# Sigmoid attention and a SiLU layer on one core: later loads for batch 3, a ring of three v tiles, and other places for scores

## The chip, the core and the metric

The kernel runs on one core of a Trainium2 chip. The metric is the device time of one execution in microseconds (us); the median of three runs of the kernel before is 384.71 us (383.19 to 385.27). Engines are named as in the profile: PE (TensorE), PEld (its weight loads), DVE (VectorE), ACT (ScalarE), POOL (GpSimd), SP (SyncE). POOL and SP only issue DMAs here, but for a few small set-up operations.

## The reference

q, k, v are float32 of shape (8, 12, 448, 64): batch, heads, sequence, head size. w_in is (768, 2048), w_out (2048, 768).

```
scores = q @ k^T / sqrt(64) - log(448)
attn   = sigmoid(scores)
x      = (attn @ v), heads put side by side: (8 * 448, 768)
h      = x @ w_in
out    = (h * sigmoid(h)) @ w_out          # (3584, 768), float32
```

## The kernel before

**Blocks and units.** The 12 heads of a batch are taken four at a time, so a batch is three blocks and all batches are 24 blocks, g = 0 to 23; batch b has blocks 3b to 3b + 2. A block has seven units, one for each chunk of 64 keys, 168 units in all. `scores` (line 171) does one unit: four matmuls of 64 rows by 64 columns of the array (psc, line 178) and one ScalarE sigmoid (attnT, line 185). PSUM holds two score tiles. `values` (line 195) multiplies a block's seven attnT tiles by v: 28 matmuls (pav, line 209) and two copies on DVE into x^T (xT, line 220).

**The layer.** `h_unit` (line 229) makes 128 of the 2048 hidden columns of a batch, called fc: six matmuls (ph), a sigmoid (tsig, line 245) and a product on DVE (gTr, line 246). `out_set` (line 286) multiplies two row blocks of gTr by w_out in seven products of eight matmuls (po, line 303) instead of eight products, by sums and differences of the operands (S on DVE, lines 315 to 323; the sums of w_out are `w_sums`, line 264). Its results go to osb tiles on DVE and from there by four stores on SP (line 296). `all_moe` (line 376) is the order of all this: h of batches 0 and 1, three sets; h of batch 2, a set, h of batch 3, two sets and one more; and so on.

**Order on PE.** There is no scheduler: instructions run in the order written. The main loop (line 528) emits a burst of two units of scores, then the values of a block if one waits, then one row copy if one is due (`rows_if_any`), then a stretch of the layer (`stretch`, line 395), which takes steps from the generator `all_moe` until their nominal nanoseconds reach what is due. Each step is one matmul. Unit n = 42 is batch 2's first, and ahead of it stands one long stretch of 21500 ns, in which h of batch 1 is done with no scores between.

**k^T and q^T.** The scores need k and q transposed. Blocks 0 to 5 are transposed on PE. From block 6 on, `dma_transpose` (line 160) copies a flat tile to rows (kr, qr) and issues a DMA transpose on SP (line 165) to kT or qT. For blocks 6 to 8 the copies are done on ACT inside h of batch 1, behind the fc units that `by_h1` (line 351) names. For later blocks they are done on DVE (line 164), one to a burst, out of the list `later` that `after_values` fills.

**Loads.** POOL issues all loads of k, q, v (`load`, line 72: two halves of 112 KB for each tensor and block), of w_in in four quarters and of w_out in four quarters, in the order in which the functions `after_transpose` (line 425) and `after_values` (line 443) call for them. A load waits on POOL until its tile is free, and all later loads stand behind it. Eight loads can be under way: each instruction also waits for the landing of the load eight places earlier. The flat tiles of k and q are rings of four, that of v a ring of five (pool p5). `load("kq", g)` in `moe_h` (line 364) and in `rows_if_any` (line 466) fetches the block four further on, right behind a transpose's copies.

Of the kernel before, what the change touches and what calls it, by code (L numbers as in the profile page):

```python
# [17 lines left out]
def kernel(  # L18
# [21 lines left out]
    NFC = DFF // P  # L40
    NO2 = DMODEL // 2
    NQB = NQ * B
# [7 lines left out]
    p2 = ctx.enter_context(tc.tile_pool(name="p2", bufs=2))  # L50
    p3 = ctx.enter_context(tc.tile_pool(name="p3", bufs=3))
    p4 = ctx.enter_context(tc.tile_pool(name="p4", bufs=4))
    p5 = ctx.enter_context(tc.tile_pool(name="p5", bufs=5))
    p12 = ctx.enter_context(tc.tile_pool(name="p12", bufs=12))
    ps_sc = ctx.enter_context(tc.tile_pool(name="ps_sc", bufs=2, space=bass.MemoryType.PSUM))
    ps_1 = ctx.enter_context(tc.tile_pool(name="ps_1", bufs=4, space=bass.MemoryType.PSUM))
# [8 lines left out]
    flat = {}  # L65

    def new_flat(name, g):
        flat[name, g] = (p5 if name == "v" else p4).tile(
            [P, 2, NCH, D], F16, tag=f"{name}f", name=f"{name}f"
        )  # L70

    def load(names, g, c0=0, c1=NCH):
        b, iq = divmod(g, NQ)
        for name in names:
            if (name, g) not in flat:
                new_flat(name, g)
            for half in range(2):
                h0 = half * (H // 2) + 2 * iq
                nc.gpsimd.dma_start(  # L79
                    flat[name, g][half * HP : (half + 1) * HP, :, c0:c1].rearrange(  # L80
                        "p i c d -> p i (c d)"
                    ),
                    source[name][b, h0 : h0 + 2].rearrange("i (p c) d -> p i (c d)", c=NCH)[
                        :, :, c0 * D : c1 * D
                    ],
                )
# [20 lines left out]
    def load_w_in(step):  # L107
        cols = slice(step * DFF // 4, (step + 1) * DFF // 4)
        nc.gpsimd.dma_start(  # L109
            w_in_sb[:, :, cols], moe_w_in[:, cols].rearrange("(cc p) f -> p cc f", p=P)  # L110
        )

    def load_w_out(nh, part):
        cols = slice(nh * NO2, (nh + 1) * NO2)
        fcs = slice(part * NFC // 2, (part + 1) * NFC // 2)
        nc.gpsimd.dma_start(
            w_out_sb[:, fcs, cols],
            moe_w_out[part * DFF // 2 : (part + 1) * DFF // 2, cols].rearrange(
                "(fc p) e -> p fc e", p=P
            ),  # L120
        )
# [104 lines left out]

    pairs = [half * NQ + iq for iq in range(NQ - 1) for half in range(2)] + [NQ - 1, 2 * NQ - 1]

    def h_unit(b, fc):
        ph = ps_1.tile([P, 512], F32, tag="ps1", name="ph")  # L230
        for at, cc in enumerate(pairs):
            assert b in ready or at < 4
            nc.tensor.matmul(  # L233
                ph[:, :S],
                w_in_sb[:, cc, fc * P : (fc + 1) * P],
                xT[b][:, cc, :],
                start=(at == 0),
                stop=(at == NCC - 1),
            )
            if at < NCC - 1:  # L240
                yield 189
        if fc == NFC - 1:
            h_done.add(b)
        tsig = p3.tile([P, S], F16, tag="tsig", name="tsig")
        nc.scalar.activation(tsig, ph[:, :S], AF.Sigmoid, bias=0.0, scale=ISX)  # L245
        nc.vector.tensor_mul(  # L246
            gTr[:, fc, (b % 2) * S : (b % 2) * S + S], ph[:, :S], tsig
        )
        yield 189
# [34 lines left out]
        return [rows_of[2 * m + u // NCH, u % NCH] for u in (2 * g, 2 * g + 1)]  # L284

    def out_set(a1, rows1, a2, rows2, last=False):
        lo, hi = slice(0, NHC), slice(NHC, NFC)
        osb = [p4.tile([P, DMODEL], F32, tag="osb", name="osb") for _ in range(2)]
        c11, c12 = (osb[0][:, nh * NO2 : (nh + 1) * NO2] for nh in range(2))
        c21, c22 = (osb[1][:, nh * NO2 : (nh + 1) * NO2] for nh in range(2))  # L290
        m1 = p2.tile([P, NO2], F32, tag="m1", name="m1")
        sg = [cpool.tile([P, NHC, P], F16, tag=f"S{i}", name=f"S{i}") for i in range(1, 5)]

        def store(rows, o, cols, engines):
            for at, (row, eng) in enumerate(zip(rows, engines)):
                eng.dma_start(row[:, cols], o[at * HP : (at + 1) * HP, cols])

        left, right, whole = slice(0, NO2), slice(NO2, DMODEL), slice(0, DMODEL)

        def product(a, w):  # L300
            po = ps_1.tile([P, 512], F32, tag="ps1", name="po")
            for fc in range(NHC):
                nc.tensor.matmul(  # L303
                    po[:, :NO2], a[:, fc, :], w[:, fc, :], start=(fc == 0), stop=(fc == NHC - 1)
                )
                if fc < NHC - 1:
                    yield 163
            return po[:, :NO2]

        def plus(o, po, x, sign=ISX):  # L310
            nc.vector.scalar_tensor_tensor(  # L311
                out=o, in0=po, scalar=sign, in1=x, op0=ALU.mult, op1=ALU.add
            )

        nc.vector.tensor_sub(sg[2], a1[:, lo], a2[:, lo])  # L315
        nc.vector.tensor_add(sg[0], a2[:, lo], a2[:, hi])
        po = yield from product(a1[:, lo], wq[0][0])
        nc.scalar.activation(m1, po, AF.Copy, scale=ISX)  # L318
        nc.vector.tensor_sub(sg[1], sg[0], a1[:, lo])
        yield 163  # L320
        po = yield from product(a1[:, hi], wq[1][0])
        plus(c11, po, m1)
        nc.vector.tensor_sub(sg[3], a1[:, hi], sg[1])
        if last:
            store(rows1, osb[0], left, (nc.sync, nc.sync))
        yield 163
        po = yield from product(sg[2], tw[3])
        plus(c22, po, m1)
        yield 163
        po = yield from product(sg[1], tw[2])  # L330
        plus(c22, po, c22)
        plus(c12, po, m1)
        yield 163
        po = yield from product(a2[:, hi], tw[4])
        plus(c21, po, c22, -ISX)
        yield 163
        po = yield from product(sg[0], tw[1])
        plus(c22, po, c22)
        plus(c12, po, c12)
        store(rows2, osb[1], whole, (nc.sync, nc.sync))  # L340
        yield 163
        po = yield from product(sg[3], wq[1][1])
        plus(c12, po, c12)
        if last:
            store(rows1, osb[0], right, (nc.sync, nc.scalar))
        else:
            store(rows1, osb[0], whole, (nc.sync, nc.sync))
        yield 163


    by_h1 = {4: 6, 7: 7, 10: 8}
    early = [h_unit(0, fc) for fc in range(2)]
    sums = w_sums()

    def moe_h(b):
        for fc in range(NFC):
            yield from early[fc] if b == 0 and fc < 2 else h_unit(b, fc)
            if b == 1:
                if fc >= 2:
                    next(sums)  # L360
                if fc in by_h1:
                    for name in ("k", "q"):
                        dma_transpose(by_h1[fc], name, act_copy)
                    load("kq", by_h1[fc] + 4)

    def moe_set(m, g):
        step = out_set(block(g), row_blocks(m, g), block(g + 1), row_blocks(m, g + 1))
# [25 lines left out]
    done = due = 0.0  # L393

    def stretch(ns):
        nonlocal done, due
        due += ns
        while done < due:
            step_ns = next(stream, None)
            if step_ns is None:  # L400
                break
            done += step_ns
# [19 lines left out]
    units = [(g, ch) for g in range(NQB) for ch in range(NCH)]  # L422
    waiting = []

    def after_transpose(g):
        if g == 0:
            load("kq", 4)
            load_w_in(1)
        elif g == 1:
            load("kq", 5)  # L430
            load_w_in(2)
            load("v", 3)
            load_w_in(3)
            load("v", 4)
        elif g == 4:
            load("kq", 8)
            load("v", 6)
            load("v", 7)
        elif g == 5:
            load("v", 8)  # L440
            load("kq", 9)

    def after_values(g):
        if g == 0:
            load("v", 5)
            for nh in range(2):
                for part in range(2):
                    load_w_out(nh, part)
        elif g == 2:
            load("kq", 6)  # L450
            load("kq", 7)
        elif g >= 4 and g + 5 < NQB:
            load("v", g + 5)
        if g >= 6:
            for to in (9, 10) if g == 6 else (g + 4,):
                if to < NQB:
                    later.extend(((to, "k"), (to, "q")))

# [2 lines left out]
    def rows_if_any():  # L461
        if later:
            g, name = later.pop(0)
            dma_transpose(g, name, nc.vector.tensor_copy)
            if name == "q" and g + 4 < NQB:
                load("kq", g + 4)

    def values_if_any():
# [110 lines left out]
```

## Time and profile before

| what | value |
|---|---|
| median of three runs | 384.71 us |
| the profiled execution: time / span | 386.89 / 385.1 us |
| granted TensorE clock | 1.000 |
| PE busy / ACT / DVE / POOL | 373.2 / 240.1 / 233.5 / 93.0 us |
| matmuls ph, po (four forms of operands and kept), psc, pav | 768, 784, 672, 672 |
| DMA queue 0 (POOL's loads) / queue 1 (SP's) | 22.69 MB / 19.31 MB |
| DMA transposes on SP | 36, kT landing after 7.5 us, qT after 7.0 us (medians) |
| POOL's longest wait in total | vf behind PE pav, 98.2 us in 12 |

The span runs from the first to the last instruction; the time of the profiled execution is a little longer. "Busy" of PE counts modelled ends of pipelined matmuls. The chain of work that ended last follows back, from the last instruction, to what released each step; a DMA in it was waited for. In a timeline, the brackets at a line's end tell how long the engine was idle and who ended it, and a trailing q ("SPq") marks an issue, not work. The DMA share is the mean busy share of 16 DMA engines; it passes 1 where packets overlap.

### The profile page before, as it was taken

Reading aid. Unit: us, or ns where it says so; the run is one execution under the profiler, and the core shown is the slowest. Engines: PE = TensorE matmul, PEld = TensorE weight load, DVE = VectorE, ACT = ScalarE, POOL = GpSimd, SP = SyncE. Lnnn points to the kernel's source line nnn. Section 1 sums busy time; section 2 is a strip of 40 time slices with the busy share of each in tenths; the row PEclk is TensorE's granted clock in tenths of the full one; section 3 lists DMA queues with packets and bytes.
Section 4 is the critical chain, followed back from the end, with each engine's and each line's share of the span. In section 5 each row is a group of like instructions: output and inputs, shape, how many; then the busy total and the mean of one; then the engine's idle time right before and its main releaser. Section 6 shows DMA issues by size and latency. Waiting matters only on the chain.

```text
span 385.1 us, 7662 instructions
## 1 busy us (share of the span) xinstructions
PE 373.2 (97%) x3083; PEld 186.8 (48%) x3083; DVE 233.5 (61%) x415; ACT 240.1 (62%) x328; POOL 93.0 (24%) x158
## 2 busy tenths in 40 slices
PE   7998999997999999999999999999999999999995
PEld 2543445553544444444555444544455444555663
DVE  2445646894685656655767546745757444756774
ACT  4998685856766886678454587577874686044000
POOL 8953516541344313221312301101000000000000
PEclk9999999999999999999999999999999999999999
DMA  7999999999999999928949764445131300110233
GB/s 111 181 190 205 205 203 170 153 130 119 195 108 210 147 212 112 171 53 98 98 107 201 68 137 73 39 115 73 24 69 40 83 3 0 26 57 2 67 98 82
DMA packets 66403, 42.71 MB, mean 111 GB/s; under 512 B 37056, under 2 KB 62912, under 8 KB 66368
## 3 DMA queue, kind: packets, MB, share of 16 engines
q0 software_dynamic: 28032, 22.69, 45.0%
q1 hardware_dynamic: 38112, 19.31, 30.1%
q8 instruction: 24, 0.39, 0.4%
q10 hardware_dynamic: 224, 0.23, 0.2%
q14 instruction: 11, 0.09, 0.1%
HBM read 45.61 MB, written 11.01 MB: 147 GB/s over the span
## 4 chain that ended last, share of the span: by engine, by line
PE 83%; DMA 8%; ACT 5%; POOL 1%; issue 1%; DVE 1%; ACTq 0%; POOLq 0%
PE ph L233 36%; PE po L303 31%; PE psc L178 9%; PE pav L209 7%; ACT attnT L185 5%; DMA qT<-qr 4%; DMA vf<-in_v_dram 3%; DMA kf<-in_k_dram 1%; POOL qf L79 1%; DVE gTr L246 0%; ACT tsig L245 0%; PE ptrk L149 0%; POOL w_in_sb L109 0%; DVE S L315 0%; POOL vf L79 0%
## 5 line engine op out<-in xcount | busy, mean ns | idle before, releaser
L185 ACT ACTIVATE attnT<-psc,bias_s 128x896 f16<-128x896 f32 x168 | 159.1, 1015 | 57.7 <-PE psc L178 57.7
L233 PE MATMUL ph<-xT,w_in_sb 128*128 128x448 f16 x768 | 153.6, 353 | 0.0
L246 DVE TENSOR_TENSOR gTr<-ph,tsig 128x448 f16<-128x448 f32 x128 | 78.1, 623 | 75.3 <-ACT tsig L245 74.5
L233 PEld LDWEIGHTS <-w_in_sb 128*128 128x128 f16 x768 | 71.8, 98 | 76.2 <-issue 13.6
L245 ACT ACTIVATE tsig<-ph 128x448 f16<-128x448 f32 x128 | 68.2, 545 | 49.9 <-PE ph L233 49.0
L303 PEld LDWEIGHTS <-S 128*128 128x128 f16 x448 | 42.1, 98 | 34.5 <-issue 6.7
L79 POOL DMA_DIRECT2D vf<-in_v_dram x48 | 28.7, 615 | 104.7 <-PE pav L209 98.2
L311 DVE SCALAR_TENSOR_TENSOR osb<-po,osb 128x384 f32<-128x384 f32 x70 | 37.7, 555 | 26.7 <-PE po L303 26.1
L178 PE MATMUL psc<-qT,kT 64*64 64x448 f16 x672 | 50.4, 362 | 3.5 <-DMA qT<-qr 2.1
L220 DVE TENSOR_SCALAR xT<-pav 128x448 f16<-128x448 f32 x48 | 27.7, 620 | 30.9 <-PE pav L209 30.9
L303 PE MATMUL po<-T,S 128*128 128x384 f16 x224 | 40.7, 327 | 0.5 <-DVE S L315 0.5
L303 PEld LDWEIGHTS <-gTr 128*128 128x128 f16 x304 | 28.8, 98 | 23.5 <-issue 4.3
L303 PE MATMUL po<-w_out_sb,S 128*128 128x384 f16 x224 | 39.9, 326 | 0.0
L209 PE MATMUL pav<-attnT,vf 64*64 64x448 f16 x672 | 38.3, 350 | 1.7 <-DMA vf<-in_v_dram 1.2
L79 POOL DMA_DIRECT2D qf<-in_q_dram x48 | 28.8, 611 | 35.6 <-DVE qr L164 10.9
L303 PE MATMUL po<-w_out_sb,gTr 128*128 128x384 f16 x192 | 34.4, 326 | 0.2 <-DVE gTr L246 0.2
L79 POOL DMA_DIRECT2D kf<-in_k_dram x48 | 28.7, 606 | 20.5 <-DMA w_out_sb<-in_moe_w_out_dram 6.1
L178 PEld LDWEIGHTS <-kT 64*64 64x64 f16 x672 | 14.9, 104 | 34.1 <-issue 33.1
L209 PEld LDWEIGHTS <-vf 64*64 64x64 f16 x672 | 20.2, 107 | 14.0 <-DMA vf<-in_v_dram 1.9
L311 DVE SCALAR_TENSOR_TENSOR osb<-po,m 128x384 f32<-128x384 f32 x42 | 23.2, 552 | 3.5 <-PE po L303 3.1
L303 PE MATMUL po<-T,gTr 128*128 128x384 f16 x112 | 21.4, 326 | 0.0
L318 ACT ACTIVATE m<-po 128x384 f32<-128x384 f32 x14 | 6.9, 493 | 21.4 <-PE po L303 21.4
(40 smaller groups left out, 131.0 us busy)
## 6 DMA issues: line engine op xcount, KB each, us to landing
out_dram<-osb SPq DMA_DIRECT2D x54, 192.0 KB, 3.4
qf<-in_q_dram POOLq DMA_DIRECT2D x48, 112.0 KB, 7.3
vf<-in_v_dram POOLq DMA_DIRECT2D x48, 112.0 KB, 4.7
kf<-in_k_dram POOLq DMA_DIRECT2D x46, 112.0 KB, 7.6
w_in_sb<-in_moe_w_in_dram POOLq DMA_DIRECT2D x4, 768.0 KB, 10.8
w_out_sb<-in_moe_w_out_dram POOLq DMA_DIRECT2D x4, 768.0 KB, 15.3
kT<-kr SPq DMA_TRANSPOSE x18, 7.5
qT<-qr SPq DMA_TRANSPOSE x18, 7.0
```

What stands on the lines that cost most here:

```text
L79: nc.gpsimd.dma_start(flat[name, g][half * HP : (half + 1) * HP, :, c0:c1].rearrange("p i c d -> p i (c d)"), source[name][b, h0 : h0 + 2] ...
L178: nc.tensor.matmul(psc[own, j, :S], qkT["k", g][rows, ch, own], qkT["q", g][rows, :, own], start=True, stop=True,)
L185: nc.scalar.activation(attnT[g, ch], psc[:, :, :S], AF.Sigmoid, bias=bias_s, scale=QKSCALE)
L209: nc.tensor.matmul(pav[half][j * D : (j + 1) * D, :S], flat["v", g][own, j, ch, :], at[own, j, :], start=(ch == 0), stop=(ch == NCH - 1),)
L220: nc.vector.tensor_scalar_mul(xT[b][:, half * NQ + iq, :], pav[half][:, :S], SX)
L233: nc.tensor.matmul(ph[:, :S], w_in_sb[:, cc, fc * P : (fc + 1) * P], xT[b][:, cc, :], start=(at == 0), stop=(at == NCC - 1),)
L245: nc.scalar.activation(tsig, ph[:, :S], AF.Sigmoid, bias=0.0, scale=ISX)
L246: nc.vector.tensor_mul(gTr[:, fc, (b % 2) * S : (b % 2) * S + S], ph[:, :S], tsig)
L303: nc.tensor.matmul(po[:, :NO2], a[:, fc, :], w[:, fc, :], start=(fc == 0), stop=(fc == NHC - 1))
L311: nc.vector.scalar_tensor_tensor(out=o, in0=po, scalar=sign, in1=x, op0=ALU.mult, op1=ALU.add)
L318: nc.scalar.activation(m1, po, AF.Copy, scale=ISX)
```

## The change

Five things are different.

1. v's flat tiles are a ring of three (pool p3) instead of five.
2. The loads stand elsewhere. v of block 3 is loaded once values(0) has been issued, ahead of the third quarter of w_in; v of blocks 4 and 5 behind values(1) and values(2), each ahead of two quarters of w_out; then v of block g + 3 behind values(g). k and q of blocks 9 to 12 are all loaded behind values(6), after v of block 9; before, they were loaded with block 5's transposes (9) and behind the copies in h of batch 1 (10 to 12).
3. The copies for the transposes of blocks 6, 7 and 8 stand behind fc 3, 6 and 9 of h of batch 1 instead of 4, 7 and 10.
4. The DVE row copies of block 9 and 10 are put into `later` behind values(7) instead of values(6), and from there on block g + 3 behind values(g) instead of g + 4.
5. A flag `hold` is set while the last fc unit of an h stage (batch 1 and on) is under way and cleared in the first product of the set that follows; while it is set, `stretch` goes on past what is due.

```
-        flat[name, g] = (p5 if name == "v" else p4).tile(
+        flat[name, g] = (p3 if name == "v" else p4).tile(
...
     def h_unit(b, fc):
+        nonlocal hold
+        hold = b > 0 and fc == NFC - 1
...
         po = yield from product(a1[:, lo], wq[0][0])
         nc.scalar.activation(m1, po, AF.Copy, scale=ISX)
         nc.vector.tensor_sub(sg[1], sg[0], a1[:, lo])
+        hold = False
         yield 163
...
-    by_h1 = {4: 6, 7: 7, 10: 8}
+    by_h1 = {3: 6, 6: 7, 9: 8}
...
                         dma_transpose(by_h1[fc], name, act_copy)
-                    load("kq", by_h1[fc] + 4)
...
-        while done < due:
+        while done < due or hold:
...
     def after_transpose(g):
...
         elif g == 1:
             load("kq", 5)
-            load_w_in(2)
-            load("v", 3)
-            load_w_in(3)
-            load("v", 4)
         elif g == 4:
             load("kq", 8)
-            load("v", 6)
-            load("v", 7)
-        elif g == 5:
-            load("v", 8)
-            load("kq", 9)
 
     def after_values(g):
         if g == 0:
+            load("v", 3)
+            load_w_in(2)
+            load_w_in(3)
+        elif g == 1:
+            load("v", 4)
+            load_w_out(0, 0)
+            load_w_out(0, 1)
+        elif g == 2:
             load("v", 5)
-            for nh in range(2):
-                for part in range(2):
-                    load_w_out(nh, part)
-        elif g == 2:
+            load_w_out(1, 0)
+            load_w_out(1, 1)
             load("kq", 6)
             load("kq", 7)
-        elif g >= 4 and g + 5 < NQB:
-            load("v", g + 5)
-        if g >= 6:
-            for to in (9, 10) if g == 6 else (g + 4,):
+        elif g + 3 < NQB:
+            load("v", g + 3)
+        if g == 6:
+            for to in (9, 10, 11, 12):
+                load("kq", to)
+        if g >= 7:
+            for to in (9, 10) if g == 7 else (g + 3,):
                 if to < NQB:
                     later.extend(((to, "k"), (to, "q")))
...
-            if name == "q" and g + 4 < NQB:
+            if name == "q" and g + 4 < NQB and g + 4 > 12:
                 load("kq", g + 4)
```

On PE the order of instructions differs only at four ends of h stages. Written as runs of matmuls: at batch 2's end, "psc 8, pav 28, ph 13, psc 8, ph 2, po 14, psc 8, po 15" becomes "psc 8, pav 28, ph 15, po 8, psc 8, po 6, psc 8, po 15"; at batch 6's end, the last with scores, "psc 8, ph 16, psc 8, ph 1, po 17, pav 28" becomes "psc 8, ph 17, po 8, psc 8, po 9, pav 28".

More of the change, by code (lines that the diff above doesn't have):

```diff
@@ L52 @@
     p4 = ctx.enter_context(tc.tile_pool(name="p4", bufs=4))
-    p5 = ctx.enter_context(tc.tile_pool(name="p5", bufs=5))
     p12 = ctx.enter_context(tc.tile_pool(name="p12", bufs=12))
@@ L286, in out_set @@
     def out_set(a1, rows1, a2, rows2, last=False):
+        nonlocal hold
         lo, hi = slice(0, NHC), slice(NHC, NFC)
@@ L319, in out_set @@
         nc.vector.tensor_sub(sg[1], sg[0], a1[:, lo])
+        hold = False
         yield 163
```

## The prediction

> **What bounds the kernel now.** I read the page's busy shares first, then the chain of work that ended last, then the waits.
>
> ```profile
> span 385.1 us, 7662 instructions
> PE 373.2 (97%) x3083; PEld 186.8 (48%) x3083; DVE 233.5 (61%) x415; ACT 240.1 (62%) x328; POOL 93.0 (24%) x158
> ```
>
> TensorE is busy 97% of the span and works its instructions strictly in order, so the change is worth the PE time that it frees or adds; no matmul is added or removed. The chain, in order of time, shows where PE stood still:
>
> ```profile
> 28.28 10.48 DMA vf<-in_v_dram
> 38.76 0.04 issue
> 38.80 1.51 PE pav L209 x26
> ...
> 74.68 17.24 DMA qT<-qr
> 91.92 0.14 issue
> 92.05 0.38 PE psc L178 x4
> ...
> 324.49 0.89 ACT attnT L185
> 325.38 0.01 issue
> 325.38 0.55 ACT tsig L245
> ```
>
> Three places, then: PE waits near 37 to 39 us for v of block 3 (batch 1's first), near 90 to 92 us for q^T of block 7, a DMA transpose that took 17.24 us, and near 326 us for a sigmoid that stands behind two others. The rest of the chain after 92 us is PE throughout. Blocks are counted g = 0 to 23, three to a batch.
>
> **Gain 1: v of block 3 ahead of w_in's third quarter.** The 28 value matmuls of block 3 would start 0.2 us after the eighth score matmul of the burst begun at 36.61, at 37.0, and take 1.32 us with no wait (the chain's pav pieces): end 38.4. They ended at 40.31. Gain 1.9 us, the same as PEld's wait for vf (1.9 us in 2 waits). v now stands ahead of a quarter of 768 KB; at the 205 GB/s of the page's slices that is 3.8 us, so v lands near 35.0, ahead of 37.0. The quarter slips by the two v halves (about 1.2 us) to 38.8; its first user, ph of fc 8, is the 49th ph matmul, near 44 us before and 42 us now: hidden with 3 us to spare. v of blocks 4 and 5 and the w_out quarters only change places; the last bytes stay near 60 us and the first w_out difference on DVE starts at 65.05 (63 now): hidden. If that cover were gone, PE would lose what is late, at most 1.2 us.
>
> **Gain 2: the stall on block 7.** The loads of k and q 9 to 12 and v 9 leave the h stage of batch 1. In 70 to 92 us the DMA share is 1.47 and the six transposes of blocks 6 to 8 run among these loads. Now only k, q 8 and v 6 to 8 come before them, issued by about 68; POOL then stands at v 9, which waits for values(6). The ScalarE copies (0.94 us each) come one unit earlier (6 ph, 1.17 us), 63.7 instead of 66.65 with gain 1 in. Block 7's q then has 20 us and an almost empty ring until its scores. The second four score matmuls would have followed at 89.81 and started at 92.05: gain 2.2 us. Next in line, block 8 (landed 99.7, used 103.6), is earlier too.
>
> **Gain 3: no scores at the end of an h stage.** The order of instructions changes at the ends of batches 2, 4, 5 and 6. Only batch 6's end, the last with scores, lost time before: two po matmuls start 0.51 and 0.60 us after the one ahead instead of 0.17, on gTr and S behind the sigmoid behind two attnT (the chain at 324 to 327). Now ph 1 and po 8 go ahead of the scores: gain 0.8. At batch 2's end the new order is psc 8, po 6, psc 8: 0.5 + 0.2 + 1.0 = 1.7 us between bursts, where two sigmoids take 1.91 us and start 0.4 after the burst does. With two score tiles, the second unit waits until 2.3 to 2.5 and wanted 1.97: loss 0.5 us. At the other two ends po 11 or more stands between: nothing.
>
> **The ring of three itself.** From v 10 on, load(g+3) waits for values(g); it lands 2.7 to 4.2 us after issue (vf at 261 us) and is used 21 units later, over 30 us: nothing.
>
> **The cost: block 9.** Its k and q loads are behind v 9, thus behind values(6); and its row copies, on DVE at values(6) before, now begin at values(7). I count in the clock of before; the whole of this stage moves by the gains together.
>
> ```profile
> 103.99 1.49 PE L209 MATMUL pav<-attnT,vf 64*64 64x448 f16 x28
> ...
> 105.52 1.16 DVE L220 TENSOR_SCALAR xT<-pav 128x448 f16<-128x448 f32 x2 [2.40 <-PE pav L209]
> ...
> 106.59 0.61 DVE L164 COPY qr<-qf 128x896 f16<-128x896 f16 x1
> ...
> 109.91 0.61 DVE L164 COPY kr<-kf 128x896 f16<-128x896 f16 x1
> ...
> 112.75 0.57 PE L178 MATMUL psc<-qT,kT 64*64 64x448 f16 x8
> ```
>
> These are values(7), and the burst with units 62 and 63; unit 63 is block 9's first, so PE needs both transposes of block 9 at 113.0. In the new order k 9's copy stands exactly where the copy at 106.59 stands, and q 9's where the one at 109.91 stands (two S subtractions ahead of it). So the k transpose is issued at 107.3 and the q copy ends at 110.5. On SP the four stores of the set just ended stand between them (osb is complete at 108.8; 2.5 us of issue), so the q transpose is issued near 111.5. Before, they were issued at 98.10 and 99.66 and landed by 110.9, 2 us ahead of need. Behind the waiting score matmul stands all of PE, and behind PE everything.
>
> How long from the k issue to the q landing is not shown for this load; by rows:
> - Alone, a transpose lands 2.9 us after issue (the least in the view of qT); from 110.5 that is 113.4: stall 0.4 us, the low end.
> - The same shape on SP later, k, four stores, q:
>
> ```profile
> 215.93 1.93 SPq L165 DMA_TRANSPOSE kT<-kr  x1
> 217.95 2.48 SPq L296 DMA_DIRECT2D out_dram<-osb  x4
> 220.53 1.35 SPq L165 DMA_TRANSPOSE qT<-qr  x1
> ```
>
> q landed 6.8 us after its issue, 11.4 after k's: 118.7 here, stall 5.7. Six load halves were about.
> - Under heavy loads, k at 104.12 and q at 107.46 (landing 13.8 us later): 17.1 us; 124.4 here, stall 11.4, the high end.
>
> Here 13 halves compete: about five of the 18 that v 9 and k, q 9 to 12 issue from 96.7 on, 0.58 us each, two of v 10, and k, q 13 and k 14. Seven more than in the second row, at 0.58 us, are 4 us; I charge somewhat over half, as some come too late to be ahead: stall 8, nearer the third row than the first.
>
> A transpose took 2.9 us alone and 17.24 among loads. [...]
>
> **Sum.** -1.9 - 2.2 - 0.8 + 0.5 + 8.0 = +3.6 us. The profiled execution has a span of 385.1 and took 386.89, 2.2 above the median 384.71 of the runs; I add to the median: **388.3 us**. Later transposes gain slack with the stall (block 10's copies at 112 and 113 don't wait for the scores, needed at 126 and more), so the stall is paid once.
>
> **Rivals.** 0.5% is 1.9 us, about what a measurement of this kernel can tell from no change.
> - *Block 9 is only as late as the second row says* (5.7): +1.3, 386.0. For it: the loads had a free ring from 96.7 on. Against: more halves than there. Chance 0.25, for stalls of 2.7 to 6.5.
> - *Block 9's transposes pass nearly undisturbed* (stall 1.6): -2.8, **381.9, faster**. The mechanism is an empty DMA at 107 us, since stores and loads of the stage drained early; it decides below a stall of 2.7, that is, a q landing before 115.7, 4 us after its issue. Against: four stores of 192 KB on the same queue directly in front. Chance 0.14.
> - *The heavy row or worse, or the change doesn't do what it says*: block 7 still waits as other transfers are its cause, or block 10 is late too: +7 and over, 391.7 to 394. Against: the loads do leave that stage. Chance 0.08.
> - The forecast, stalls of 6.5 to 11: 0.53.
>
> Faster by over 0.5%: 0.14; within: 0.25; slower: 0.61. The range leaves out most of the third case's far side and of the second's: 382.0 to 392.5.
>
> **What would show it.** No DMA vf wait at 37 us; no qT wait near 88; a wait of PE's psc for DMA qT of about 8 us near 109 (new clock), with SP's order k transpose, four stores, q transpose before it; no tsig in the chain at batch 6's end; PE otherwise as before. Wrong if the wait near 109 is under 3 us, or a second one follows at block 10 or 11.

## The result, and the profile after

The changed kernel takes 396.21 us (median of six runs, 395.49 to 396.81) where the kernel before, run beside it, takes 384.34 us (383.19 to 387.79): the ratio is 1.030, with an interval of 1.025 to 1.034. The forecast was 388.3 us, in a range up to 392.5. The sign was right, the size was not: +11.9 us where +3.6 were forecast. The profiled execution took 395.73 us with a span of 394.0 us; the mean granted clock of TensorE in it is 0.986.

From the page of the changed kernel, first the span and busy times, then two rows of the 40 slices (one digit for each 9.85 us):

```profile
span 394.0 us, 7664 instructions
...
PE 374.2 (95%) x3083; PEld 187.9 (48%) x3083; DVE 233.8 (59%) x415; ACT 240.1 (61%) x328; POOL 93.0 (24%) x158
...
PE   7999999999907999999999999999999999999995
...
PEclk9999999999977999999999999999999999999999
```

PE has 1.0 us more of busy time than before and 8.9 us more of span. Both stand in the main in one place: the twelfth slice (108 to 118 us) has almost no work on PE, and in it and the next the clock was lower. The chain of work that ended last passes through that place so (start, duration, what):

```profile
103.31 5.10 DMA qf<-in_q_dram
108.41 12.03 DMA qT<-qr
120.44 0.14 issue
120.58 0.59 PE psc L177 x4
121.16 3.18 PE po L307 x12
```

The forecast had a wait of PE's scores for block 9's q^T "of about 8 us near 109". It is there, behind the first four matmuls of the burst begun at 108.9, and takes 11.3 us (waits by line: us in total, times, longest):

```profile
PE psc L177 <- DMA qT<-qr: 11.3, 1, 11.3
```

SP's queue before it has the order that was forecast (start and duration of the issues, the number at the end counts them):

```profile
103.41 1.23 SPq L164 DMA_TRANSPOSE kT<-kr  x1
104.73 3.58 SPq L300 DMA_DIRECT2D out_dram<-osb  x4
108.41 1.61 SPq L164 DMA_TRANSPOSE qT<-qr  x1
```

k's transpose is issued at 103.41 and lands at 111.01. Behind it come four stores, and then q's transpose, issued at 108.41. The DMA records in the trace place its packets at 113.33 to 119.0, and it has landed at 120.44. From k's issue to q's landing that is 17.0 us, while the score matmul wanted it at about 109.2.

The chain holds a second loss: 12 po matmuls took 3.18 us, where 12 take 2.06 in the chain of before. In the windows around the wait (length; busy time and instructions of PE, PEld, DVE, ACT, POOL; granted clock; DMA share; GB/s) the clock stands at a half from about 4 us into the wait until 2.8 us after it:

```profile
105.00:109.00 4.00, 4.00 (x33) 1.97 (x31) 4.00 (x8) 3.31 (x5) 2.52 (x5) 1.00 1.20 148
109.00:113.20 4.20, 0.28 (x4) 0.01 (x3) 0.85 (x2) 1.01 (x1) 2.38 (x4) 1.00 1.24 258
113.20:120.50 7.30, 0.00 (x0) 0.00 (x0) 0.00 (x0) 0.00 (x0) 0.00 (x0) 0.50 1.29 183
120.50:123.40 2.90, 2.83 (x12) 1.29 (x13) 0.80 (x2) 1.01 (x1) 0.00 (x0) 0.50 0.36 78
123.40:134.00 10.60, 10.60 (x96) 5.17 (x95) 5.72 (x11) 6.43 (x8) 3.54 (x6) 1.00 0.68 106
```

Four score matmuls (0.59 instead of 0.38 us) and the 12 of po make 1.3 us of it.

The two waits that the change was forecast to take away are gone. In the timeline of PE the values of block 3 stand directly behind the scores (before, in the profiled execution, they ended at 40.31):

```profile
37.01 0.57 PE L177 MATMUL psc<-qT,kT 64*64 64x448 f16 x8
37.41 1.49 PE L208 MATMUL pav<-attnT,vf 64*64 64x448 f16 x28
```

No wait for q^T of block 7 is left near 88 us: the transposes of blocks 6 to 8 have all landed by 79.6 us. At batch 6's end the chain no longer holds a tsig. At batch 2's end a new small wait appears, as forecast, and a little larger. The chain there:

```profile
153.94 1.31 PE po L307 x8
155.25 0.02 issue
155.28 0.49 ACT m L322
155.77 1.80 ACT attnT L184 x2
157.57 0.04 issue
157.61 0.38 PE psc L177 x4
158.00 2.06 PE po L307 x12
```

The first burst starts at 155.17; eight scores, six po and eight scores are 2.03 us by the rows of before, so the next po was due at 157.20 and came at 158.00: 0.8 us. The forecast counted 0.5, as it had both sigmoids start 0.4 us after the burst; the first of them stands behind the layer's copy m on ACT and starts 0.6 us after it.

Against the profiled execution of before the terms are: wait +11.3, clock +1.3, batch 2's end +0.8, batch 6's end -0.8, block 3 -1.9, block 7 -2.2: +8.5 of a difference of 8.9 us in span. The other 0.4 stand ahead of block 3, whose burst begins at 37.01 instead of 36.61.

### The profile page after: what moved, and what is told of

Its sections match the earlier page's. It is cut to its first block, busy times and chain, and to the rows that moved or that the text cites. A ratio compares the mean times of both kernels' runs of the same rounds, so it can differ in the third digit from the quotient of the medians.

```text
span 394.0 us, 7664 instructions
## 1 busy us (share of the span) xinstructions
PE 374.2 (95%) x3083; PEld 187.9 (48%) x3083; DVE 233.8 (59%) x415; ACT 240.1 (61%) x328; POOL 93.0 (24%) x158
## 4 chain that ended last, share of the span: by engine, by line
PE 73%; DMA 16%; POOL 3%; ACT 3%; DVE 2%; issue 2%; DVEq 0%; POOLq 0%
PE po L307 29%; PE ph L236 28%; PE psc L177 8%; PE pav L208 6%; DMA w_in_sb<-in_moe_w_in_dram 6%; DMA w_out_sb<-in_moe_w_out_dram 4%; DMA qT<-qr 3%; DMA qf<-in_q_dram 2%; POOL kf L78 1%; DVE gTr L249 1%; POOL qf L78 1%; DMA ks<-in_k_dram 1%; ACT attnT L184 1%; ACT qr L138 1%; DVE T L278 1%
## 5 line engine op out<-in xcount | busy, mean ns | idle before, releaser
L177 PE MATMUL psc<-qT,kT 64*64 64x448 f16 x672 | 50.8, 363 | 13.5 <-DMA qT<-qr 11.3
## 6 DMA issues: line engine op xcount, KB each, us to landing
w_out_sb<-in_moe_w_out_dram POOLq DMA_DIRECT2D x4, 768.0 KB, 17.1
```

Source lines behind the costliest of these rows:

```text
L177: nc.tensor.matmul(psc[own, j, :S], qkT["k", g][rows, ch, own], qkT["q", g][rows, :, own], start=True, stop=True,)
```

## The experiments

Theory A after the result: the wait is block 9's own. Its copies stand one block later, at values(7), which leaves too little time; the stores ahead of its q transpose and the loads beside it make it long. Rival B: the loads that the ring of three holds back, and that then run as one bunch, cost the time wherever the copies stand. A third question was the clock. All kernels but three (those that start from before, and say so) are the changed kernel with one edit or more, and ratios are against the kernel before, run on the same chip.

**Block 9's copies back at values(6).** Its loads stand again with block 5's transposes; ring of three, `hold` and all else stay.

```
         elif g == 4:
             load("kq", 8)
+        elif g == 5:
+            load("kq", 9)
...
-            for to in (9, 10, 11, 12):
+            for to in (10, 11, 12):
...
-        if g >= 7:
-            for to in (9, 10) if g == 7 else (g + 3,):
+        if g >= 6:
+            for to in (g + 3,):
```

> The changed kernel, but k and q of block 9 are loaded with block 5's transposes (as before the change) and its two row copies follow values(6) instead of values(7); block 10's copies follow values(7); the loads of 10 to 12 stay behind values(6). Theory A (the loss is block 9's transposes being issued one block too late): the 11.6 us wait goes, with the half clock after it, and the gains stay: about 381 to 383 us. Rival B (the DMA queues as a whole are overloaded once the loads are put behind values(6)): the wait moves to block 10 or 11 and the time stays over 389.

Measured: 382.62 us (382.37 to 382.95, nine runs), ratio 0.994 [0.992, 0.996]. SP's timeline:

```profile
94.26 1.22 SPq L164 DMA_TRANSPOSE kT<-kr  x1
95.82 1.52 SPq L164 DMA_TRANSPOSE qT<-qr  x1
...
104.74 2.74 SPq L300 DMA_DIRECT2D out_dram<-osb  x4
```

The transposes are issued 9 and 13 us earlier, back to back, and land at 101.7 and 103.9, 5 us ahead of need. No wait for q^T is left, and no half clock near it. The spans differ by 12.8 us (394.0 and 381.2), the wait and the clock by 12.6. Rival B falls: the ring of three and the bunch of loads, but for block 9's four halves, are still there, and no wait comes of them once block 9 is early. The edit that lost the time is the fourth of the change (what goes into `later`, and when), with the loads that belong to it.

**What makes the wait 11 us long.** Five kernels leave the copies at values(7) and take away one neighbour or two.

*Loads of blocks 11 and 12 behind block 9's q copy*, instead of at values(6):

```
-            for to in (9, 10, 11, 12):
+            for to in (9, 10):
...
+            if name == "q" and g == 9:
+                load("kq", 11)
+                load("kq", 12)
```

> The changed kernel, but the eight load halves of k and q 11 and 12 are issued behind block 9's q copy instead of behind values(6). Theory A1 (the loads in front of and beside block 9's transposes make up most of their time): 8 halves at 0.58 us leave the queue ahead of them, and q of block 9 lands 4 to 6 us earlier: 390 to 392 us. Rival A2 (the stores on SP's queue between the two transposes make the delay, loads little): within 1.5 us of the changed kernel's 396.2.

Measured: 396.3 us (395.47 to 396.63), ratio 1.029 [1.025, 1.032], a wait of 12.2 us. This tells nothing of the loads, since POOL's timeline shows them going out at once, still beside the transposes:

```profile
102.82 1.21 POOL L78 DMA_DIRECT2D kf<-in_k_dram  x2
103.98 1.23 POOL L78 DMA_DIRECT2D qf<-in_q_dram  x2
105.15 1.25 POOL L78 DMA_DIRECT2D kf<-in_k_dram  x2
106.32 1.27 POOL L78 DMA_DIRECT2D qf<-in_q_dram  x2
```

*The four stores behind block 9's q transpose on SP:*

```
+    def out_set(a1, rows1, a2, rows2, last=False, put_off=None):
...
+            if put_off is not None:
+                put_off.append((rows, o, cols, engines))
+                return
...
+            put_off=late if (m, g) == (0, 2) else None,
...
+            if (g, name) == (9, "q"):
+                for rows, o, cols, engines in late:
+                    for at, (row, eng) in enumerate(zip(rows, engines)):
+                        eng.dma_start(row[:, cols], o[at * HP : (at + 1) * HP, cols])
```

> The changed kernel, but the four stores of the set that ends there are issued on SP behind block 9's q transpose instead of ahead of it. Rival A2 (stores on the same queue): the q transpose is issued about 2 us earlier and passes 768 KB less: 4 to 5 us gained, 391 to 392. Theory A1 (loads): under 2 us gained, since the transposes still share the engines with the loads, 394 or more.

Measured: 392.8 us (391.56 to 394.19), ratio 1.021 [1.017, 1.026]. SP's timeline and PE's wait:

```profile
103.20 1.22 SPq L164 DMA_TRANSPOSE kT<-kr  x1
106.49 1.30 SPq L164 DMA_TRANSPOSE qT<-qr  x1
107.84 3.22 SPq L481 DMA_DIRECT2D out_dram<-osb  x4
```

```profile
PE psc L177 <- DMA qT<-qr: 7.0, 1, 7.0
```

q is issued 1.9 us earlier and its first packet comes 3.3 us after the issue instead of 4.9. Its packets still take 5.6 us (109.78 to 115.40). Without the stores in front the wait is 4.3 us shorter.

*The loads of blocks 13 to 16 later*, out of the way of block 9's transposes:

```
-            if name == "q" and g + 4 < NQB and g + 4 > 12:
+            if name == "q" and g in (11, 12):
+                load("kq", 2 * g - 9)
+                load("kq", 2 * g - 8)
+            elif name == "q" and g + 4 < NQB and g + 4 > 16:
```

> The changed kernel, but k and q of blocks 13 and 14 are loaded behind block 11's copies, and 15 and 16 behind block 12's, so that no load is issued beside block 9's q transpose after v of block 10. The earlier run only moved loads from ahead of the transposes to beside them; this one takes eight halves out of that stretch. Theory A1 (a transpose that shares the engines with loads takes 5 to 6 us instead of about 1): q of block 9 lands 4 to 6 us earlier, 390 to 392 us. Rival A2 (the stores in front of it alone): under 1.5 us gained, 395 or more.

Measured: 390.63 us (390.16 to 391.64), ratio 1.014 [1.010, 1.017]:

```profile
PE psc L177 <- DMA qT<-qr: 5.8, 1, 5.8
```

The stores are back in front, but q's packets take 2.5 us (111.68 to 114.19), with the fourth store's beside them and no load's behind 111.1. Without the loads of 13 and 14 beside q's transpose the wait is 5.5 us shorter.

*Both:*

> The changed kernel with both earlier edits at once: the four stores behind block 9's q transpose, and the loads of 13 to 16 behind later copies. Theory A (wait = what stands in front on SP's queue + what shares the engines): alone they left 7.3 and 6.1 us of 11.6; together about 2 us are left, too short for the half clock, 385 to 386.5 us. Rival (one of the two causes contains the other): 5 us or more left, 389 or more.

Measured: 388.39 us (387.17 to 389.74, ten runs), ratio 1.006 [1.003, 1.010]. The expectation was missed in both of its numbers. The wait:

```profile
PE psc L177 <- DMA qT<-qr: 3.9, 1, 3.9
```

q is issued at 106.54, PE wants it 2.6 us later, and it lands 6.3 us after its issue. With the least landing time of a q transpose in the profiles of the kernels before and after, 2.9 us, the wait would be an estimated 0.3 us, so the late start alone does not make the 3.9. k's packets (105.76 to 109.03) stand right ahead of q's (109.32 to 112.31), and the loads of blocks 9 to 12 are under way until 108.3, v of block 10 until 112.2. And the half clock came all the same, from just before the wait's end:

```profile
109.00:112.30 3.30, 0.12 (x4) 0.00 (x0) 0.70 (x2) 1.01 (x1) 0.00 (x0) 1.00 1.38 128
112.30:119.10 6.80, 6.11 (x36) 2.69 (x40) 1.58 (x3) 1.94 (x3) 0.00 (x0) 0.50 0.58 178
119.10:129.00 9.90, 9.90 (x83) 4.63 (x75) 5.21 (x10) 6.50 (x10) 5.95 (x10) 1.00 0.85 122
```

6.11 us of PE's work ran at half clock, so 3.0 us were lost behind a wait of 3.9. This execution is the longest of the ten: six of the others have a mean clock of 0.994 to 0.996 where it has 0.991, and take 387.2 to 388.4 us.

*v's ring of five again*, so that the loads are not held back:

```
-        flat[name, g] = (p3 if name == "v" else p4).tile(
+        flat[name, g] = (p5 if name == "v" else p4).tile(
```

> The changed kernel with v's ring of five again, and nothing else undone: v of blocks 9 and the loads behind it on POOL's queue no longer wait for values(6), while block 9's copies still follow values(7). Theory A with A1: the loads of 9 to 12 are over before block 9's transposes, whose wait shrinks to 4 to 7 us: 388 to 392 us; or, if the copies' place alone decides, 396 as the changed kernel. The wait for block 7 may come back in part (0 to 2.2 us of this).

Measured: 392.77 us (391.57 to 393.83), ratio 1.019 [1.015, 1.023]:

```profile
PE psc L178 <- DMA qT<-qr: 6.3, 1, 6.3
```

The loads of blocks 9 to 12 then run at 68 to 92 us, beside the transposes of blocks 6 to 8 (the last of them lands at 93.96 instead of 79.6), and are no longer beside block 9's. So the ring of three itself takes part: it is what puts these loads into block 9's way, worth 5.0 us of the wait, about as much as the loads of 13 to 16. The time falls by 3.4 us only, as the half clock lasts to 121.13 and PE starts again at 115.14: 6.0 us at half clock, 3.0 us lost.

**The clock.** 46 matmuls on constant tiles are put ahead of block 9's first score, to keep PE busy in the wait; they add work and change no result.

```
         for u in burst:
+            if u == (9, 0):
+                keep_busy(46)
             scores(*u)
```

> The changed kernel with 46 matmuls of constants (about 0.215 us each, 9.9 us) put ahead of block 9's first scores, inside the wait, so that TensorE stays busy. Theory C (the idle wait itself halves the granted clock, from 4 us after it begins to 2.8 us after it ends): the clock stays at 1.0 and 1.4 us are gained, 394.8. Without C: the same time as the changed kernel, 396.2, or up to 0.5 more.

Measured: 393.9 us (393.57 to 397.03), ratio 1.024 [1.021, 1.028]: 2.3 us less than the changed kernel's median, where 1.4 were expected. The profiled execution is the longest of the six and can't carry that difference; in it the wait was longer than the dummies. PE's timeline:

```profile
108.51 10.10 PE L135 MATMUL pw<-dummy 128*128 128x512 f16 x46
121.66 0.59 PE L177 MATMUL psc<-qT,kT 64*64 64x448 f16 x4 [3.04 <-DMA qT<-qr]
```

PE was idle for 3.0 us only and the half clock lasted from 121.51 to 124.92. The other five take 393.6 to 394.3 us at a mean clock of 0.998 to 1.000, where the changed kernel has 0.983 to 0.987: there the half clock is gone. That it costs about 1 to 2 us behind the changed kernel's wait is shown; the exact size is not.

**The gains by themselves.** The kernel before, unchanged, once more:

> The kernel before, unchanged, for a second profile of it: if block 7's wait of 2.2 us and block 3's of 1.9 us are there in each execution, all three gains hold against the median; if block 7's wait is absent or smaller here, the profiled execution of before was a long one because of it, and gain 2 was counted on a wait that most executions don't have.

Measured: 384.93 us (383.24 to 388.53, eight runs), ratio 1.001 [0.998, 1.005]. Its profiled execution is the shortest of them, 383.24 us, and has neither the wait for v of block 3 nor that for q^T of block 7. From PE's timeline:

```profile
36.77 0.57 PE L178 MATMUL psc<-qT,kT 64*64 64x448 f16 x8
37.17 1.70 PE L209 MATMUL pav<-attnT,vf 64*64 64x448 f16 x28
```

Gains 1 and 2 thus stand in some executions and not in others, and the profile that the prediction read (386.89 us) was one that had both. Of four profiles in which the loads behind block 7 stand as before (these two and those of the next two kernels), only that one has block 7's wait. For gains 1 and 3 two kernels tell what they are worth at the median; gain 2 has no run of its own.

*Before, with v of block 3 alone ahead of w_in's third quarter:*

```
+            load("v", 3)
             load_w_in(2)
-            load("v", 3)
             load_w_in(3)
```

> The kernel before with v of block 3 ahead of the third quarter of w_in, and nothing else. If block 3's wait of 1.9 us stood in most executions, the median falls by 1.5 to 1.9 us. If it stands only in some (the second profile of before has none of it), the median falls by 0 to 0.7 us.

Measured: 383.1 us (382.57 to 384.97, twelve runs), ratio 0.995 [0.992, 0.997]. Gain 1 is real at the median: 2.0 us, between 1.0 and 3.0 by the interval.

*Before, with `hold` from batch 4 on alone* (`hold = b > 3 and fc == NFC - 1`):

> The kernel before with the flag that holds scores back, from batch 4 on, and nothing else. Theory: only batch 6's end loses time before (0.8 us), so 0.8 us are gained, median 0.5 to 1.2 under before's. Rival: the late scores cost ScalarE what PE gains: no difference.

Measured: 384.03 us (382.68 to 386.42, twelve runs), ratio 0.998 [0.995, 1.000]. The time alone does not resolve it. In its profile the loss at batch 6's end falls from 0.8 or 0.9 us to 0.1.

**A version that beats both.** Block 9 early, and `hold` from batch 4 on, which spares batch 2's end:

```
-        hold = b > 0 and fc == NFC - 1
+        hold = b > 3 and fc == NFC - 1
```

> The kernel with block 9 early (382.6), and the flag that holds scores back set from batch 4 on only, so that batch 2's end has its former order. Theory: the two bursts of scores that stand 1.7 us apart there cost 0.8 us and the former order cost nothing: 381.8 us. Rival (the wait is taken up later): 382.6.

Measured: 381.69 us (381.35 to 382.05, six runs), ratio 0.990 [0.987, 0.993], 0.9 us below the one with block 9 early alone. Its page:

```profile
span 379.8 us, 7665 instructions
...
PE 371.4 (98%) x3083; PEld 186.5 (49%) x3083; DVE 233.7 (62%) x415; ACT 239.8 (63%) x328; POOL 93.3 (25%) x158
```

*The same with v's ring of five:*

> The best version so far (block 9 early, flag from batch 4 on: 381.7 us, within 0.7 us of each other) with v's ring of five again, so that the loads of 10 to 12 are no longer held behind values(6). Theory D (holding these loads back is what keeps block 7's transposes free of waits): the wait for block 7 comes back in some executions, the median is 382 to 384 and the runs lie up to 3 us apart. Rival: the gate does nothing, 381.7 with the same narrow spread.

Measured: 382.06 us (381.61 to 384.63, twelve runs), ratio 0.992 [0.989, 0.994]. The median is 0.4 us higher, which the intervals do not resolve, and three of the twelve runs take 382.7 to 384.6, where all six of the other's lie within 0.7 us. Holding the loads back may matter in some executions only, which would be what is left of gain 2; the profile of this kernel (382.1 us) has no wait for block 7, and none of the three long runs was profiled.

## Why the prediction was wrong

- **The bound** was right: PE's order sets the end, and the microseconds in which it waited or ran slowly are in the time (12.6 of the 12.8 us between the spans of the changed kernel and the one with block 9 early).
- **Gain 1** (-1.9) was right: -2.0 at the median (1.0 to 3.0), by the run that has this edit alone. That one execution showed just the size of the median is in part luck, as another had no such wait.
- **Gain 2** (-2.2) was right in the profile it was read from and is not shown as a term of the median: the other three profiles lack the wait, and the ring of five against three gives about -0.4, not resolved.
- **Gain 3** (-0.8) is seen in the profiles, and the loss at batch 2's end is 0.8 to 0.9 instead of 0.5, so `hold` over all batches brings nothing.
- **The ring of three itself, "nothing"**, held for what it was said of: PE does not wait for a load of v in the changed kernel's profile. The ring's other effect, that it holds the loads of blocks 9 to 12 back to block 9's transposes, was counted under block 9; with a ring of five the wait there is 5.0 us shorter.
- **The cost: block 9.** This is the step that failed. Place, cause and SP's order were as forecast, but "stall 8" measured 11.3. By the forecast q was issued 4.2 us after k and landed 9.5 us later; measured are 5.0 and 12.0. The term was set between two rows by counting load halves at 0.58 us each and charging "somewhat over half" of them. The runs show that half the issue time was too little: without the eight halves of 13 and 14 beside q's transpose its packets took 2.5 instead of 5.7 us, and the wait fell by 5.5 us, 0.7 a half. It fell by 5.0 without the loads of 9 to 12 about, and by 4.3 without the stores in front. These parts don't add up (7.4 with the stores and the loads of 13 to 16 away at once), and what the last 3.9 us consist of is not shown. The high end, 17.1 us from k's issue to q's landing, is almost the measured 17.0, but by luck. It is the row of block 10 in the profile of before, and no store stands between its k and q; block 9's two transposes stand in front instead:

```profile
98.10 1.22 SPq L165 DMA_TRANSPOSE kT<-kr  x1
99.66 4.36 SPq L165 DMA_TRANSPOSE qT<-qr  x1
104.12 3.25 SPq L165 DMA_TRANSPOSE kT<-kr  x1
107.46 2.80 SPq L165 DMA_TRANSPOSE qT<-qr  x1
```

- **A term was missing**: the half clock after the wait, +1.3 us in the profile.
- **The sum** mixed two things: terms read from one execution, which was 2.2 us above the median because it had the waits of gains 1 and 2, were added to the median. With the medians' figures for the gains, and the wait and clock of the profile, the sum is -2.0 - 0.4 - 0.8 + 0.8 + 11.3 + 1.3 = +10.2 us; +11.9 was measured. About 1.0 of the last 1.7 us is that the profiled execution was a short one: the changed kernel's median is 13.6 us above that of the kernel with block 9 early, where the profiles show 12.6 of wait and clock. Four of its six executions have a mean clock of 0.983 (395.8 to 396.8 us), the other two, the profiled one among them, 0.986 and 0.987 (395.73 and 395.49); 0.983 fits one more stretch of 3.41 us at half clock, as the profile of the kernel with the loads of 11 and 12 later shows it, with a wait of 12.2. The other 0.7 is open.
- **The rivals.** The faster one fell, as its "empty DMA at 107 us" was a share of 1.20 to 1.29. The third, "the heavy row or worse", with a chance of 0.08, was the one that came, by its size; the reasons named for it, that block 7 still waits or that block 10 is late too, did not.

Not tried: stores on another queue than SP's, and the ring of five together with the stores behind and the loads of 13 to 16 later, which would show what the late start costs with all its neighbours away.

## What to carry to other kernels

When a step moves behind a later event, look for a row that has the same neighbours both in the queue and among the transfers under way. Here there was none: k, four stores, q with six load halves about took 11.4 us, and 17.0 where 13 halves were counted. A price between two rows, made up from the issue time of loads, was too low; without such a row the range should reach past the heaviest one. A wait seen in one profiled execution is a gain at the median only if other executions have it too, so take a second profile of the kernel before crediting it. A prefetch whose slack is 2 us, as block 9's was before, has none to give: look for the one-line edit that leaves it where it was, and keep the rest of the change.

## What the hardware showed

The half clock came in stretches of one length and its multiples, by the clock records of the profiled executions (in brackets the mean granted clock of each): 3.41 us (dummies in the wait, 0.995), 6.83 (stores behind; loads 13 to 16 later; both; 0.991 each), 10.24 (changed kernel, 113.17 to 123.41 us, 0.986; ring of five, 0.987) and 13.65 (loads 11 and 12 later, 0.982). The wait for block 7 in the profile of before, 2.1 us of idle PE, did not bring it (granted clock 1.00 in the windows from 87 to 96 us); one of 3.0 us at the end of the dummies did, and one of 3.9 us cost 3.0 more. The length of the wait alone does not tell the price: behind the wait of 3.9 us 6.1 us of PE's work ran at half clock, behind the one of 11.3 only 2.8. What sets it is not shown.

How long the packets of a DMA transpose of 224 KB took went with what moved beside them: 0.8 us with no load moving (block 7's q in the changed kernel, 74.19 to 75.02), 2.5 beside one store and no load (block 9's q with the loads of 13 to 16 later, 111.68 to 114.19), 5.7 beside loads (block 9's q in the changed kernel, 113.33 to 119.0). That the transposes share engines with the loads, as theory A1 has it, was the author's explanation; the runs show the times.
